# Nyström attention feeding a top-1 expert layer: attention's instruction order written out by hand, and the pseudo-inverse on 32x32 diagonal tiles

## Chip, cores, metric

One core of a Trainium2 chip runs the whole program in one launch. The metric is the device time in microseconds from launch to end; the median of several runs is compared. A profile of one execution shows what each engine did: TensorE (PE, with its weight loads apart as PEld), VectorE (DVE), ScalarE (ACT), GpSimd (POOL), SyncE (SP) and the DMA queues.

## What is computed

Attention for 8 batches, 8 heads, 576 tokens, head size 64, in f32, with 32 "landmarks" (means of 18 consecutive tokens), then a layer of 8 experts where each token goes to one.

```python
q_lm = q.reshape(B, H, 32, 18, D).mean(axis=3)      # k_lm likewise
A  = sm(q, k_lm); Bm = sm(q_lm, k_lm); C = sm(q_lm, k)   # softmax of scaled products
Z = Bm.T / (norm1(Bm) * norm_inf(Bm) + 1e-6)
for _ in range(6):
    Z = 2 * Z - Z @ Bm @ Z
x = A @ Z @ C @ v                                    # rows of 512: 8 heads x 64
logits = x @ w_gate;  e = argmax(logits)
out = softmax_prob(e) * sigmoid(x @ w_output_gate)[e] * (relu(x @ w1[e]) @ w2[e])
```

## The kernel before

**Units of work.** A batch is split into two halves of four heads (`hf`), so that 4 heads x 32 landmarks fill 128 partitions. There are 16 such half-batches, called units below. The program is written as a plain loop over batches and halves (L209, L213); the framework's scheduler decides in which order each engine gets the instructions, interleaving batches as buffers allow.

**Loads and turning (`turned`, L175 to L194).** q and k of a unit come by one DMA each on SP's queue (L178) into one of three buffers `nats` that borrow the space of the last expert's weights; v comes by three DMAs (L216). DVE turns the 32x32 blocks (L180). POOL sums 18 tokens to a landmark in five adds (L181 to L186) and spreads the landmarks with a mask into a block-diagonal matrix `bd` (L191), so that one 128x128 matmul serves four heads.

**Scores (`scores`, L196 to L207)**: four matmuls of 288 columns for C (L246) and for A (L268).

**Softmaxes.** C: maximum (L247), exponential on ACT (L250), transposes of the result (L257), copies (L258), times v (L262, 32-column tiles). A: DVE transpose out of PSUM (L270), maximum (L272), POOL subtracts (L276), ACT exponential (L277), DVE sum and reciprocal (L278, L279), POOL multiplies (L280), DVE transposes back into `AT` (L282). B: L225 to L243, with POOL writing it block-diagonal into `XW` (L235).

**Pseudo-inverse (L291 to L308).** Z is kept multiplied with C v: `XW` has, for each half, 128 columns of block-diagonal matrix and 64 of values, and seven steps each do one matmul of 192 columns per half (L295) and one DVE instruction (L299, L303, L306).

**Routing and output.** Z times the gate weights (L317 to L334), choice of expert (L336 to L350), ranks by counting (L353 to L368), a one-hot table `St` (L369), coefficients (L375 to L386). Token rows `x` come from ten matmuls of 256 columns per batch (L393), an ACT copy to bf16 (L396) and a store to DRAM (L397). Then positions are inverted into a list `gat_i` (L400 to L450).

**Expert weights** (`load_expert`, L75 to L82) are loaded by POOL's queue in f32 and cast to bf16 on the way, two DMAs an expert: expert b after batch b (b < 6), experts 6 and 7 after the last `AT`, because their space is borrowed till then.

**Experts (L452 to L522).** 43 tiles of 128 tokens: gather by an indirect DMA on POOL's queue (L464), transposes (L469), 8 matmuls (L483), ReLU (L487), transposes (L493), 8 matmuls (L502), scaling (L508), scatter (L509).

Of the kernel before, what the change touches and what calls it, by code (L numbers as in the profile page):

```python
# [22 lines left out]
F32 = mybir.dt.float32  # L23
BF16 = mybir.dt.bfloat16
EXP = mybir.ActivationFunctionType.Exp
SIG = mybir.ActivationFunctionType.Sigmoid
RELU = mybir.ActivationFunctionType.Relu
# [9 lines left out]
def kernel(  # L37
# [98 lines left out]
    s_bm = scale / (g * g)  # L136
    s_a = scale / g
    s_c = scale / g
    KC = g // 2
    NC = KC * m  # L140
    VJ = 6
    VA = g // VJ

    with tc.tile_pool(name="attn_c", bufs=1) as cp, \
# [17 lines left out]
        for G in Gs:  # L162
# [4 lines left out]
        nats = [wall[:, E - 1, i * 2 * GD:(i + 1) * 2 * GD].bitcast(F32).rearrange("p (k d) -> p k d", d=D)  # L167
                for i in range(3)]
        t9 = wall[:, E - 1, 6 * GD:7 * GD].bitcast(F32).rearrange("p (k d) -> p k d", d=D)
        VD = HH * VJ * D  # L170
        vSs = [wall[:VA * m, E - 2, i * 2 * VD:(i + 1) * 2 * VD].bitcast(F32).rearrange(
            "p (h j d) -> p h j d", h=HH, j=VJ) for i in range(2)]
        turns = iter(range(4 * B))

        def turned(src, b, hf):  # L175

            nat = nats[next(turns) % 3]
            nc.sync.dma_start(out=nat, in_=src[b, hf * HH:(hf + 1) * HH].rearrange("h (r k) d -> (h r) k d", k=g))  # L178
            tr = sb.tile([128, g, 2, m], F32, tag="tr", bufs=3)
            nc.vector.transpose(out=tr.rearrange("p k c r -> p (k c r)"), in_=nat.rearrange("p k d -> p (k d)"))  # L180
            nc.gpsimd.tensor_tensor(t9, nat[:, 0:9], nat[:, 9:18], op=ADD)  # L181
            nc.gpsimd.tensor_tensor(t9[:, 0:4], t9[:, 0:4], t9[:, 4:8], op=ADD)
            nc.gpsimd.tensor_tensor(t9[:, 0:2], t9[:, 0:2], t9[:, 2:4], op=ADD)
            nc.gpsimd.tensor_tensor(t9[:, 0], t9[:, 0], t9[:, 1], op=ADD)
            lm = sb.tile([128, D], F32, tag="lm")
            nc.gpsimd.tensor_tensor(lm, t9[:, 0], t9[:, 8], op=ADD)  # L186
            lmT = sb.tile([128, 2, m], F32, tag="lmT", bufs=4)
            nc.vector.transpose(out=lmT.rearrange("p c r -> p (c r)"), in_=lm)
            bd = sb.tile([128, 2, HH, m], F32, tag="bd", bufs=4)
            for c in range(2):  # L190
                nc.gpsimd.tensor_tensor(  # L191
                    bd[:, c], mask,
                    lmT[:, c, :].rearrange("p (h r) -> p h r", h=1).to_broadcast([128, HH, m]), op=MUL)
            return tr, lmT, bd  # L194

        def scores(bd, tr, tag, by_j=False):  # L196

            p = ps.tile([128, 2, 512], F32, tag=tag)
            for n in range(2):
                for c in range(2):  # L200
                    if by_j:
                        rhs = tr.rearrange("p (a j) c r -> p j a c r", j=VJ)[:, n * VJ // 2:(n + 1) * VJ // 2, :, c, :]
                    else:
                        rhs = tr[:, n * KC:(n + 1) * KC, c, :]
                    nc.tensor.matmul(p[:, n, :NC], lhsT=bd[:, c].rearrange("p h r -> p (h r)"),  # L205
                                     rhs=rhs, start=(c == 0), stop=(c == 1))
            return p[:, :, :NC]  # L207

        for b in range(B):  # L209
            XW = sb.tile([128, 2, 128 + D], F32, tag="X", bufs=3)  # L210
            cc = sb.tile([128, 2], F32, tag="cc")
            ATs = []
            for hf in range(2):  # L213
                vS = vSs[hf]
                for a in range(VA):
                    nc.sync.dma_start(  # L216
                        out=vS[a * m:(a + 1) * m],
                        in_=v[b, hf * HH:(hf + 1) * HH].rearrange("h (r k) d -> r h k d", k=g)[:, :, a * VJ:(a + 1) * VJ, :])
                qT, qlmT, qBD = turned(q, b, hf)
                kT, klmT, kBD = turned(k, b, hf)  # L220


                pB = ps.tile([128, 192], F32, tag="m", bufs=2)
                for c in range(2):
                    nc.tensor.matmul(pB[:, :m], lhsT=qBD[:, c].rearrange("p h r -> p (h r)"),  # L225
                                     rhs=klmT[:, c, :], start=(c == 0), stop=(c == 1))
                st = sb.tile([128, 8], F32, tag="st", bufs=4)
                nc.vector.tensor_reduce(st[:, 0:1], pB[:, :m], axis=X, op=MAX)
                nc.vector.tensor_scalar(out=st[:, 1:2], in0=st[:, 0:1], scalar1=-s_bm, scalar2=None, op0=MUL)
                Bm = sb.tile([128, m], F32, tag="Bm")  # L230
                nc.scalar.activation(out=Bm, in_=pB[:, :m], func=EXP, scale=s_bm, bias=st[:, 1:2],
                                     accum_out=st[:, 2:3])
                nc.vector.reciprocal(st[:, 3:4], st[:, 2:3])
                nc.vector.tensor_scalar(out=Bm, in0=Bm, scalar1=st[:, 3:4], scalar2=None, op0=MUL)
                nc.gpsimd.tensor_tensor(  # L235
                    XW[:, hf, :128].rearrange("p (h r) -> p h r", r=m), mask,
                    Bm.rearrange("p (h r) -> p h r", h=1).to_broadcast([128, HH, m]), op=MUL)
                pS = ps.tile([128, 192], F32, tag="m", bufs=2)
                nc.tensor.matmul(pS[:, :m], lhsT=bones, rhs=Bm)
                nc.vector.tensor_reduce(cc[:, hf:hf + 1], pS[:, :m], axis=X, op=MAX)  # L240
                nc.vector.tensor_scalar(out=cc[:, hf:hf + 1], in0=cc[:, hf:hf + 1], scalar1=1e-6,
                                        scalar2=None, op0=ADD)
                nc.vector.reciprocal(cc[:, hf:hf + 1], cc[:, hf:hf + 1])  # L243


                pC = scores(qBD, kT, "sc", by_j=True)  # L246
                nc.vector.tensor_reduce(st[:, 4:5], pC, axis=mybir.AxisListType.XY, op=MAX)  # L247
                nc.vector.tensor_scalar(out=st[:, 5:6], in0=st[:, 4:5], scalar1=-s_c, scalar2=None, op0=MUL)
                EC = sb.tile([128, VJ, VA * m], F32, tag="EC", bufs=1)
                nc.scalar.activation(out=EC.rearrange("p (n j) q -> p n (j q)", n=2), in_=pC, func=EXP,  # L250
                                     scale=s_c, bias=st[:, 5:6], accum_out=st[:, 6:7])
                nc.vector.reciprocal(st[:, 7:8], st[:, 6:7])
                ECT = sb.tile([VA * m, VJ, 128], F32, tag="ECT", bufs=1)
                for j3 in range(2):
                    pE = ps.tile([VA * m, VJ // 2, 128], F32, tag="et")
                    for j in range(VJ // 2):
                        nc.tensor.transpose(pE[:, j, :], in_=EC[:, j3 * (VJ // 2) + j, :], identity=I128)  # L257
                    nc.scalar.copy(ECT[:, j3 * (VJ // 2):(j3 + 1) * (VJ // 2), :], pE)  # L258
                pV = ps.tile([128, 192], F32, tag="m", bufs=2)
                for j in range(VJ):  # L260
                    for h in range(HH):
                        nc.tensor.matmul(pV[h * m:(h + 1) * m, :D], lhsT=ECT[:, j, h * m:(h + 1) * m],  # L262
                                         rhs=vS[:, h, j, :], start=(j == 0), stop=(j == VJ - 1))
                nc.vector.tensor_scalar(out=XW[:, hf, 128:], in0=pV[:, :D], scalar1=st[:, 7:8],
                                        scalar2=None, op0=MUL)


                pA = scores(kBD, qT, "sa")  # L268
                At = sb.tile([128, g, m], F32, tag="At")
                nc.vector.transpose(out=At.rearrange("p (n k) r -> p n (k r)", n=2), in_=pA)  # L270
                ax = sb.tile([128, 2, g], F32, tag="ax")
                nc.vector.tensor_reduce(ax[:, 0], At, axis=X, op=MAX)  # L272

                def b_l(ap):
                    return ap.rearrange("p (k r) -> p k r", r=1).to_broadcast([128, g, m])
                nc.gpsimd.tensor_tensor(At, At, b_l(ax[:, 0]), op=SUB)  # L276
                nc.scalar.activation(out=At, in_=At, func=EXP, scale=s_a)  # L277
                nc.vector.tensor_reduce(ax[:, 1], At, axis=X, op=ADD)  # L278
# [5 lines left out]
            if b < E - 2:  # L284
                load_expert(b, ATs[1])
            elif b == B - 1:
                load_expert(E - 2, ATs[1])
                load_expert(E - 1, ATs[1])
# [264 lines left out]
```

## Time and profile before

| | us |
|---|---|
| median of 3 runs (567.03 to 570.1) | 567.15 |
| the profiled execution: its time | 568.91 |
| its span, first to last instruction | 567.2 |
| PE / DVE / POOL / ACT busy in it | 438.5 / 285.8 / 305.1 / 122.0 |
| first expert transpose (L469) starts | 371.8 |

The profile has a line for each group of instructions: the source line, engine, operation, the tiles it writes and reads, the count, the busy time, the mean of one in ns, and the idle time of the engine before it with what ended that wait. A row of the timeline gives the start, the time from the first start to the last end, and the count. A row of stretches gives each engine's busy time between two moments. "PEclk" or clock is the granted share of TensorE's full clock.

### The profile page before, as it was taken

The numbers are of one execution on the slowest core, as the hardware profiler recorded it, in microseconds if no ns is written. First come the engines' busy times: TensorE is split into PE (matmuls) and PEld (weight loads), VectorE is DVE, ScalarE is ACT, GpSimd is POOL, SyncE is SP. The second block draws the span as 40 slices with busy tenths as digits, with TensorE's granted clock in tenths as the row PEclk, the third lists the DMA queues.
The fourth block names the chain that finished last, engine by engine and source line by source line (L and its number), as shares of the span: only waits on it lengthen the run. The fifth ranks groups of instructions, "written<-read, shape, count | busy, mean of one in ns | idle before, by whom it ended". The sixth has DMA issues, their size and how long they took to land. (4 is left out here: it accounts for less than half of the span.)

```text
span 567.2 us, 9257 instructions
## 1 busy us (share of the span) xinstructions
PE 438.5 (77%) x3127; PEld 277.0 (49%) x3127; DVE 285.8 (50%) x748; ACT 122.0 (22%) x279; POOL 305.1 (54%) x492
## 2 busy tenths in 40 slices
PE   0458758758776867779797878559999999999992
PEld 0235545536555545448474554325555555555551
DVE  1355557657666756736764322713444444353441
ACT  0012222123131222122231211112223222232220
POOL 2667895796687678585624111353444545454422
PEclk9978969969897958877897565769999999999998
DMA  6643946935989369388044754121232323223200
GB/s 163 168 125 84 210 119 180 213 107 118 254 195 206 100 167 218 103 156 184 9 111 68 126 92 72 33 75 57 75 112 85 107 81 104 86 92 94 85 29 0
DMA packets 41726, 66.13 MB, mean 117 GB/s; under 512 B 10353, under 2 KB 29810, under 8 KB 41682
## 3 DMA queue, kind: packets, MB, share of 16 engines
q0 software_dynamic: 18048, 31.90, 26.3%
q1 hardware_dynamic: 23634, 33.64, 21.5%
q8 instruction: 27, 0.44, 0.4%
q14 instruction: 17, 0.14, 0.1%
HBM read 67.58 MB, written 16.56 MB: 148 GB/s over the span
## 5 line engine op out<-in xcount | busy, mean ns | idle before, releaser
L205 PE MATMUL p<-tr,bd 128*128 128x288 f32 x256 | 88.6, 474 | 28.5 <-DVE tr L180 21.1
L509 POOL DMA_INDIRECT out_dram<-ysb x43 | 43.5, 1012 | 93.7 <-DVE ysb L508 90.0
L483 PE MATMUL ph<-wall,xT 128*128 x344 | 82.9, 385 | 3.0 <-DVE xT L471 2.9
L502 PE MATMUL py<-wall,hT 128*128 x344 | 81.1, 379 | 0.0
L393 PE MATMUL pX<-ZB,AT 128*128 128x256 f32 (+1 forms) x160 | 63.4, 520 | 19.8 <-ACT xo L396 15.2
L487 ACT ACTIVATE h<-ph 128x512 bf16<-128x512 f32 x86 | 46.7, 594 | 144.7 <-PE ph L483 141.6
L205 PEld LDWEIGHTS p<-tr,bd 128*128 128x128 f32 x256 | 52.9, 222 | 41.4 <-POOL bd L191 29.7
L295 PE MATMUL pN<-nxt 128*128 128x192 f32 x192 | 47.8, 375 | 19.9 <-DVE nxt L303 16.8
L483 PEld LDWEIGHTS <-xT 128*128 128x128 bf16 x344 | 33.9, 99 | 45.3 <-issue 5.7
L393 PEld LDWEIGHTS pX<-ZB,AT 128*128 128x128 f32 (+1 forms) x160 | 32.7, 233 | 44.1 <-ACT xo L396 23.1
L181 POOL TENSOR_TENSOR wall<-wall 128x576 f32<-128x576 f32 x32 | 44.9, 1402 | 13.7 <-DMA wall<-in_q_dram 11.3
L295 PEld LDWEIGHTS pN<-nxt 128*128 128x128 f32 x192 | 34.8, 209 | 33.7 <-DVE nxt L303 26.6
L464 POOL DMA_INDIRECT xs<-x_rows,gat_i x43 | 41.9, 974 | 15.9 <-issue 13.4
L180 DVE STREAM_TRANSPOSE tr<-wall 128x1152 f32<-128x1152 f32 x32 | 43.3, 1352 | 12.4 <-DMA wall<-in_q_dram 11.5
L502 PEld LDWEIGHTS <-hT 128*128 128x128 bf16 x344 | 31.9, 98 | 30.7
L495 DVE COPY hT<-pht 128x1024 bf16<-128x1024 bf16 x43 | 29.7, 690 | 29.4 <-PE pht L493 23.2
L507 DVE CAST ysb<-xs 128x1 int32<-128x1 f32 x43 | 6.6, 154 | 74.7 <-issue 64.6
L191 POOL TENSOR_TENSOR bd<-mask,lmT 128x128 f32<-128x128 f32 x64 | 28.0, 456 | 25.2 <-PE p L205 11.8
L508 DVE TENSOR_SCALAR ysb<-py,xs 128x512 f32<-128x512 f32 x43 | 31.9, 743 | 4.2 <-PE py L502 3.8
L396 ACT CAST xo<-pX 128x512 bf16<-128x512 f32 (+1 forms) x40 | 23.3, 581 | 49.9 <-PE pX L393 34.4
L303 DVE SCALAR_TENSOR_TENSOR nxt<-nxt,pN 128x384 f32<-128x384 f32 x40 | 21.5, 538 | 17.9 <-PE pN L295 17.7
L276 POOL TENSOR_TENSOR At<-At,ax 128x576 f32<-128x576 f32 x16 | 18.4, 1157 | 21.1 <-DVE ax L272 21.1
(136 smaller groups left out, 607.3 us busy)
## 6 DMA issues: line engine op xcount, KB each, us to landing
wall<-in_moe_w_dram POOLq DMA_DIRECT2D x16, 1024.0 KB
wall<-in_v_dram SPq DMA_DIRECT2D x48, 192.0 KB, 4.2
wall<-in_q_dram SPq DMA_DIRECT2D x16, 576.0 KB, 5.1
wall<-in_k_dram SPq DMA_DIRECT2D x16, 576.0 KB, 5.2
x_rows<-xo SPq DMA_DIRECT2D x32, 128.0 KB, 2.8
xs<-x_rows,gat_i POOLq DMA_INDIRECT x43
out_dram<-ysb POOLq DMA_INDIRECT x43
x_rows<-St SPq DMA_DIRECT2D x1, 516.0 KB, 4.6
```

Of the source, the lines that this page charges most:

```text
L180: nc.vector.transpose(out=tr.rearrange("p k c r -> p (k c r)"), in_=nat.rearrange("p k d -> p (k d)"))
L181: nc.gpsimd.tensor_tensor(t9, nat[:, 0:9], nat[:, 9:18], op=ADD)
L205: nc.tensor.matmul(p[:, n, :NC], lhsT=bd[:, c].rearrange("p h r -> p (h r)"), rhs=rhs, start=(c == 0), stop=(c == 1))
L295: nc.tensor.matmul(pN[:, hf, :], lhsT=cur[:, hf, :128], rhs=cur[:, hf, :])
L393: nc.tensor.matmul(pX[:tk, hf * HH * D:(hf + 1) * HH * D], lhsT=ATs[hf][:, j * 128:j * 128 + tk], rhs=ZB[:, hf].rearrange("p h d -> p (h d)"))
L464: nc.gpsimd.indirect_dma_start(out=xs, out_offset=None, in_=x_rows, in_offset=bass.IndirectOffsetOnAxis(ap=gat_i[:, j:j + 1], axis=0))
L483: nc.tensor.matmul(ph[hf], lhsT=xT[:, dc, :], rhs=wf[:, bass.ds(we[j] + (dc * F + hf * 512), 512)], start=(dc == 0), stop=(dc == DCH - 1))
L487: nc.scalar.activation(out=hs[j][:, hf * 512:(hf + 1) * 512], in_=ph[hf], func=RELU)
L495: nc.vector.tensor_copy(hTs[j], pht)
L502: nc.tensor.matmul(py, lhsT=hT[:, fc, :], rhs=wf[:, bass.ds(we[j] + (W1 + fc * HD), HD)], start=(fc == 0), stop=(fc == FCH - 1))
L508: nc.vector.tensor_scalar(out=ysb[:, :HD], in0=py, scalar1=xs[:, HD // 2:HD // 2 + 1], scalar2=None, op0=MUL)
L509: nc.gpsimd.indirect_dma_start(out=out, out_offset=bass.IndirectOffsetOnAxis(ap=token, axis=0), in_=ysb[:, :HD], in_offset=None, bounds_ch ...
```

## The change

1. Each step becomes a small function, and a list `plan` gives each call a place in time, in units of a period P = 12.0 a unit; the calls are sorted by place and issued under `manual_schedule`, so each engine's order is the program's. Loads of q and k are placed before those of v, for several units ahead, into six buffers (the space of experts 7 and 5); `AT` moves into seven slots of expert 4's space.
2. q and k are turned by TensorE (18 transposes a unit, `turn3`, copied by ACT, `keep3`) instead of DVE; landmarks too (`turn_lm`). The sums of q go to DVE, those of k stay on POOL. `bd` is gone.
3. Scores use 64x32 tiles: 8 matmuls of 288 columns, one per head and half of the contraction.
4. The pseudo-inverse has 96 columns a head and half (32 of matrix, 64 of values) in place of 192, with four 32x32 matmuls per half on the array's diagonal. B's softmax is done for both halves at once.
5. Experts 0 to 3 load after batches 0 to 3; experts 5, 6, 7 after the last `AT`; expert 4 last of all, after the last token rows.

The core of the diff:

```diff
+        nats = [home(E - 1 - i // 3 * 2, i % 3, GD).rearrange("p (k d) -> p k d", d=D) for i in range(6)]
+        def sums(u, i):
+            eng, t9, nat = (nc.gpsimd, nc.vector)[i], t9s[i], nats[(2 * u + i) % 6]
+            eng.tensor_tensor(t9, nat[:, 0:9], nat[:, 9:18], op=ADD)
+            eng.tensor_tensor(t9[:, 0:4], t9[:, 0:4], t9[:, 4:8], op=ADD)
+            eng.tensor_tensor(t9[:, 0:2], t9[:, 0:2], t9[:, 2:4], op=ADD)
+            eng.tensor_tensor(t9[:, 0], t9[:, 0], t9[:, 1], op=ADD)
+            lm[u, i] = sb.tile([128, 2, D], F32, tag=f"lm{i}", name="lm")
+            eng.tensor_tensor(lm[u, i], t9[:, 0:1].to_broadcast([128, 2, D]), t9[:, 8:9].to_broadcast([128, 2, D]), op=ADD)
+        def turn3(u, i, n):
...
+            tr[u, i, n] = pT = ps.tile([128, 3, 128], F32, tag="t", bufs=2, name="pT")
+            for k2 in range(3):
+                nc.tensor.transpose(pT[:, k2], identity=I128,
+                                    in_=nat[:, 6 * n + 2 * k2:6 * n + 2 * k2 + 2].rearrange("p k d -> p (k d)"))
+        def keep3(u, i, n):
+            nc.scalar.copy(tr[u, i][:, 3 * n:3 * n + 3], tr.pop((u, i, n)))
+        def scores(lms, tr, by_j=False):
+            p = ps.tile([128, 2, 512], F32, tag="s")
+            for h in range(HH):
+                for i in range(2):
+                    rhs = tr[i * D:(i + 1) * D, :, hm(h)]
...
+                    nc.tensor.matmul(p[hm(h), i, :NC], lhsT=lms[i * D:(i + 1) * D, hm(h)], rhs=rhs)
-                for hf in range(2):
-                    nc.tensor.matmul(pN[:, hf, :], lhsT=cur[:, hf, :128], rhs=cur[:, hf, :])
+        def p_mm(b, it):
+            pNs[b] = pN = ps.tile([128, 2, W + D], F32, tag="n", name="pN")
+            cur = XWs[b]
+            for hf in range(2):
+                for h in range(HH):
+                    nc.tensor.matmul(pN[hm(h), hf, :], lhsT=cur[hm(h), hf, :W], rhs=cur[hm(h), hf, :])
+        def a_back(u):
+            ATs[u] = home(E - 4, u % 7, S)
+            nc.vector.transpose(out=ATs[u], in_=Ats.pop(u).rearrange("p k r -> p (k r)"))
+        P = 12.0
+        for u in range(NU):
+            t = u * P
+            at(t - 4 * P + 11.9 if u > 2 else -30 + u, load_qk, u)
+            at(t - 2 * P + 11.9 if u > 1 else -30 + u + 0.5, load_v, u)
+            for n in range(3):
+                at(t - P + 1.5 + 0.4 * n, turn3, u, 0, n)
+                at(t - P + 2.6 + 0.5 * n, keep3, u, 0, n)
+                at(t - P + 4.9 + 0.4 * n, turn3, u, 1, n)
+                at(t - P + 5.5 + 0.5 * n, keep3, u, 1, n)
+            at(t - P + 0.1, sums, u, 0)
+            at(t - P + 1.9, sums, u, 1)
...
+            at(t + 0.0, c_scores, u)
+            at(t + 0.8, c_max, u)
+            at(t + 1.6, c_exp, u)
+            at(t + 3.5, a_scores, u)
...
+            at(t + P + 0.2, a_back, u)
...
+            for it, place in enumerate((0.7, 4.2, 7.8, 10.5, 12.7, 16.2, 19.8)):
+                at(t + place, p_mm, b, it)
+                at(t + place + 0.9, p_next, b, it)
...
+            for j, place in enumerate((6.9, 9.8, P + 2.8, P + 6.9, P + 9.7)):
+                at(t + place, x_mm, b, j)
+                at(t + place + 1.0, x_out, b, j)
+        for e in range(E):
+            u = 2 * e + 1 if e < E - 4 else NU - 1
+            at((NU + 4) * P if e == E - 4 else u * P + P + 3.3, lambda e=e, u=u: load_expert(e, ATs[u]))
+        with tc.manual_schedule():
+            for _, _, fn, args in sorted(plan, key=lambda p: p[:2]):
+                fn(*args)
```

## The prediction

> **What bounds the kernel now.** I read the page's head, then stretches of the span, then the chain's last part, then single lines.
>
> ```profile
> span 567.2 us, 9257 instructions
> 98.00:330.00 232.00, 174.31 (x1343) 123.69 (x1347) 140.85 (x391) 55.09 (x144) 145.48 (x265) 0.83 0.65 145
> 331.00:346.00 15.00, 11.19 (x43) 7.94 (x34) 3.80 (x8) 0.00 (x0) 1.70 (x2) 0.50 0.85 140
> 372.00:560.00 188.00, 181.13 (x1204) 96.68 (x1201) 78.87 (x171) 46.67 (x86) 82.09 (x84) 0.98 0.25 81
> ```
>
> The rows of stretches give from:to, length, then busy time of PE, weight loads, DVE, ACT, POOL, the granted clock, the DMA share and GB/s. From 372 us the experts run with PE busy 181 of 188 us at clock 0.98: that stage is PE-bound and the change leaves its code alone, so its 195.4 us (567.2 - 371.8, where 371.76 is its first transpose) stay. All before it is attention, and there no engine is full: in 98 to 330 PE has 75%, DVE 61%, POOL 63%, DMA 65%. The exponential of the C scores runs at 29.5 us for the first half-batch and at 321.7 for the sixteenth: 292.2 / 15 = 19.5 us of cadence, against a largest engine sum of 14.6 (0.75 x 19.5). So attention is bound by the order in which work reaches the engines, and the end by when the experts can begin.
>
> ```profile
> 165.78 0.88 PE L262 MATMUL pV<-wall,ECT 96*32 96x64 f32 x48
> 168.04 2.11 PE L205 MATMUL p<-tr,bd 128*128 128x288 f32 x8
> 342.70 1.65 PE L295 MATMUL pN<-nxt 128*128 128x192 f32 x4 [0.65 <-DVE nxt L303]
> 344.99 1.65 PE L295 MATMUL pN<-nxt 128*128 128x192 f32 x4 [0.65 <-DVE nxt L303]
> 347.02 0.47 PE L317 MATMUL pZ<-I,nxt 128*128 128x128 f32 x1 [0.38 <-DVE nxt L306]
> 371.76 0.58 PE L469 MATMUL pt<-Ib,xs 128*128 128x128 bf16 x4 [5.14 <-issue]
> ```
>
> Each f32 matmul is two instructions here. L205: 8 in 2.11 us, so 243 ns each from start to start once the last one's 0.41 us tail is taken off. L262: 48 instructions of 64 columns in 0.88 us, 14 ns each; alone, 64 of 288 columns would take 54. So four 32-column tiles run beside each other. The last three rows: an iteration of the last pseudo-inverse takes 2.29 us, and from its end to the experts lie 24.7 us.
>
> **Cadence after the change, engine by engine**, per half-batch ("unit"), each batch's work halved.
>
> *PE.* Gone: 16 score instructions (3.9 us), and half the columns of the pseudo-inverse. Added: 20 transposes of 128x128 (L257: 3 in 0.49 us, 109 ns each) = 2.2. Each of a unit's two score sets is now 16 instructions of 288 columns on 64x32 tiles: if all eight tiles run together 2 x 243 = 0.49 us, if only the four column groups do 0.97; twice a unit 1.0 to 1.9. Six transposes of EC 0.65, values 0.7. Per batch: seven iterations of 4 x 82 ns (half of L295's 163) = 2.3, token outputs 20 x 216 ns (L393) = 4.3, the small ones 1.0; half of 7.6 is 3.8. Sum 8.3 to 9.3. A change of tile shape costs: after a transpose the first L262 starts 202 ns later where the next transpose would start after 109, so 93 ns; some 22 changes a unit, 2.0 us. Total 10.3 to 11.3 at full clock, 12.4 to 13.6 at 0.83.
>
> *DVE.* The 1.35 us transposes (L180) go. Kept: L247 0.75, L270 0.77, L272 0.74, L278 0.75, reciprocals 0.4, L282 0.77 = 4.2. New: the sums of q come from POOL, five adds of 576, 256, 128, 64, 128 columns. Nearest rows with two SBUF inputs: L414 0.49 us for 320, L424 0.60 for 430; so 0.15 us + 1.05 ns a column, 1.95. Bounds: POOL's 3.4 for the same (L181 1.40 + 0.73 + 0.46 + 0.33 + 0.46), and 1.2 if the fixed part overlaps. Per batch: pseudo-inverse 2.3 (L303's 0.54 with half the columns is 0.34; six, and a last 0.28), routing lines L336 to L383 without waits 4.4, B softmax 1.5; half of 8.2 is 4.1. Sum 10.2.
>
> ```profile
> L345 DVE TENSOR_TENSOR w<-lg,sm x8: 199/439/1334, 70.0 to 352.4; 128x40 f32<-128x40 f32 x8
> L369 DVE TENSOR_TENSOR St<-row,psl x8: 806/930/1955, 84.7 to 356.8; 128x640 bf16<-128x640 f32 x8
> L181 POOL TENSOR_TENSOR wall<-wall 128x576 f32<-128x576 f32 x32 | 44.9, 1402 | 13.7 <-DMA wall<-in_q_dram 11.3 <-DMA wall<-in_k_dram 0.8
> ```
>
> Minimum/median/maximum: the same 40-column instruction takes 0.20 or 1.33 us, with POOL busy beside it, and L369 0.81 or 1.96. The longest excess, 1.15, is about one POOL instruction (L276 1.16, L181 1.40). Mean excess of L345, L349 and L369: 0.40, 0.33, 0.31, so 0.35 us per two-input instruction. The change has 8.5 of them a unit (five sums, seven per batch): 0 to 3.0 us, nearest the upper end, since sums of q and k now run side by side on the two engines. DVE: 10.2 to 13.2.
>
> The Trainium skill (SBUF — State Buffer, Who interferes with whom) says a DVE instruction with two SBUF inputs and a GpSimd instruction that reads SBUF exclude each other for their whole length. By it the 1.95 us and POOL's 3.4 us of sums add up rather than overlap, at most 1.95 us on either engine; the spread of L345 agrees. This speaks against moving a sum to DVE.
>
> *ACT* gets six copies of 384 columns (L258 0.47 each), 2.8; with L250 0.93, L277 0.68, two ECT copies 0.95, small 0.6 and half of 4.2 per batch: 8.1. *POOL* loses the bd products (4 x 0.46) and q's sums: 3.4 + 1.16 + 1.16 + half of 3.2, 7.3, and 1.0 more while experts load. *DMA* per unit: SP's queue took 21.5% of the span, 122 us, nearly all for attention: 7.6 for each of 16 units; one expert is 0.85 x 15 = 12.75 (second row above; the one expert loaded alone, 2.1 MB). Four experts in units 1 to 8: 7.6 + 6.4 = 14.0 there, 7.6 later; the loads are queued two units ahead, which covers it. SP's order changes too: token stores, for which SP now waits 133.7 us on ACT's copy, stand between loads that are wanted two units later, so a late store costs nothing up to that lead.
>
> The plan's places repeat every 12.0, but fix an order alone. So DVE about 12.5 to 13.2 and PE 11 to 13 stand level, both in fixed order: each finds its head instruction waiting at times (two PSUM tiles for all transposes: the third group of three waits for ACT's 0.47 us copy). I take 14.0 us, 94% for the fuller one; bounds 12.0 and 17.6 (13.2 at PE's present 75%).
>
> **Start, tail, sum.** First C exponential: k's load is now issued first, at 4.8 instead of 8.4; landing, sums 3.4, turning and scores give about 20 us (29.5 now). The sixteenth: 20 + 15 x 14 = 230 (321.7 now).
>
> After it, by rows, 9.6 us to the first iteration as now, seven iterations of 1.45 (2.29 less half of 4 x 0.32 at the half clock granted there, less 0.2 on DVE) = 10, then 24.7: experts at +44. But another wait is longer. The change lets experts 5, 6, 7 load only after the last AT (about +10: six DVE, POOL and ACT steps of 0.7 to 1.5), and expert 4 after the last token output. The first gather stands behind all four on POOL's DMA queue. That this queue goes in order is shown once: expert 7's two halves were issued at 331.9 and 332.7; packets of the first ran 333.4 to 339.4, of the second 339.1 to 345.0. So +10 + 1.5 + 4 x 12.75 + 3.1 (gather issue at 368.63 to L469) = +65.5. The cover which hid these loads, six of eight experts loaded during attention, is down to four.
>
> Experts begin at 20 + 15 x 14 + 65.5 = 295.5; end 295.5 + 195.4 = **491 us**. The profiled execution took 568.91 with a span of 567.2; the median of the runs is 567.15, equal to the span, so I compare spans with it.
>
> **Rivals.**
> - *The gathers do not wait for the weights* (other packets slip in, or loads run faster alone): +44 instead of +65.5, 469 us. For: DMA is only 14% busy in the tail. Against: the two halves above.
> - *Loose order*: the fuller engine reaches only 75% as now: 17.6 us, 281 + 264 = 545. For: every engine has strict order, so one late head holds all behind it.
> - *The tiles do not run side by side* (the change doesn't do what it says): 16 x 82 ns an iteration instead of 4 x 82, +0.98 us, 7 per batch, +3.4 per unit; PE 14.7, with waits 16.5: 528. For: no row shows four row groups together. Against: L262 for columns. The Trainium skill (TensorEngine Tiling (Array Packing), Restrictions and Gotchas) says different row tiles must not write one PSUM bank at a time, and pN is one bank: by it these would be taken in turn, 528, without it 491. No row before shows it.
> - *Slower: DVE blocked by POOL.* If each two-input instruction waits for a whole POOL one (1.2 us): 8.5 x 1.2 = 10.2, DVE 20.4, cadence 20.5: 588. It decides from 19.1 us ((567 - 281) / 15), that is 1.05 us per instruction. For: L345's maximum, and the sums now meet. Against: mean 0.35.
>
> **Chances.** Forecast 0.47 (12.5 to 15.5 us: 468 to 513); no wait 0.20; loose 0.13; tiles in turn 0.08; DVE blocked 0.12. A measurement can tell about 0.5% from no change. Slower: 0.10 of the last case; same 0.02 at the edge; faster 0.88. Range 450 to 548: below lies the no-wait case under 12.7 us (0.05), above half the loose case and the blocked one (0.17).
>
> **What would show it.** C exponentials 14 us apart; L345's successors with long maxima; sums on DVE near 2 to 3 us a unit; sixteen score instructions in 0.7 to 1.2 us; sixteen pN instructions in about 0.5; a DMA row near 0.85 with POOL's first gather landing only as the fourth expert ends; PE idle for some 20 us before L469's successor; then 195 us as before. Wrong if the cadence is above 16 or below 12, or if the first gather lands among weight packets.

## Result and profile after

The changed kernel takes **469.38 us** (median of 4 runs, 468.03 to 471.07) where the kernel before takes 568.62 (median of 4, 567.03 to 572.1): ratio 0.8249, 95% interval [0.8198, 0.8301]. The prediction said 491, in 450 to 548. The profiled execution took 468.03 with a span of 466.3, and the steps below are compared in spans.

The page of the changed kernel, its head and the slices of PE, the granted clock and DMA:

```profile
span 466.3 us, 11680 instructions
PE 378.6 (81%) x4401; PEld 223.2 (48%) x4423; DVE 259.6 (56%) x676; ACT 165.2 (35%) x383; POOL 227.2 (49%) x332
PE   0878877888788888887677349999999999999991
PEclk9887998999999999999775559999999999999997
DMA  6975999699797645221899950223223233323200
```

Each digit of a slice stands for 11.7 us. Read them from the left: nearly full clock through attention (the first 19 slices), then the tail, where DMA stands at 8 or 9 for four slices (20 to 23), the clock falls to 5 (22 to 24) and PE to 3 and 4 (23 and 24), then the experts as before. The stretches of the same kernel say it in microseconds (from:to, length, busy time of PE, weight loads, DVE, ACT, POOL, then clock, DMA share, GB/s; a share above 1 means that the times of the packets add up to more than the 16 engines' time):

```profile
133.00:200.00 67.00, 54.94 (x981) 35.69 (x982) 54.02 (x150) 37.63 (x98) 35.46 (x54) 1.00 0.59 155
212.00:265.00 53.00, 34.76 (x379) 21.03 (x378) 26.71 (x93) 11.44 (x30) 19.91 (x43) 0.72 0.94 167
265.00:272.00 7.00, 0.00 (x0) 0.00 (x0) 0.00 (x0) 0.00 (x0) 5.48 (x6) 0.50 1.19 242
272.00:466.00 194.00, 179.74 (x1182) 97.05 (x1204) 79.89 (x172) 46.67 (x86) 79.84 (x81) 0.97 0.24 76
```

In the steady part of attention PE and DVE now both stand at 81 to 82% and the clock at 1.00; before, 98 to 330 had 75%, 61% and 0.83. Then 53 us of tail with DMA at 0.94, and 7 us in which PE, DVE and ACT do nothing at all and POOL only issues gathers. The experts take 194 us as they did.

| step (spans, us) | before | predicted | after |
|---|---|---|---|
| first C exponential | 29.5 | 20 | 18.7 |
| 15 units of cadence | 19.5 each, 292.2 | 14.0 each, 210 | 12.87 each, 193.1 |
| sixteenth C exponential to experts | 50.1 | 65.5 | 60.4 |
| experts | 195.4 | 195.4 | 194.1 |
| sum | 567.2 | 491 | 466.3 |

Of the 100.9 us gained in span, cadence gave 99.1 and the start 10.8; the tail took 10.3 back, and the experts gave the last 1.3.

### The profile page after: what moved, and what is told of

It is laid out like the page before. It is cut to its first block, busy times and chain, and to the rows that moved or that the text cites. A ratio compares the mean times of both kernels' runs of the same rounds, so it can differ in the third digit from the quotient of the medians.

```text
span 466.3 us, 11680 instructions
## 1 busy us (share of the span) xinstructions
PE 378.6 (81%) x4401; PEld 223.2 (48%) x4423; DVE 259.6 (56%) x676; ACT 165.2 (35%) x383; POOL 227.2 (49%) x332
## 5 line engine op out<-in xcount | busy, mean ns | idle before, releaser
L210 PE MATMUL pT<-I,wall 128*128 128x128 f32 x288 | 49.7, 305 | 28.0 <-ACT tr L214 15.7
L214 ACT COPY tr<-pT 128x384 f32<-128x384 f32 x96 | 43.2, 479 | 39.7 <-PE pT L210 39.5
L210 PEld LDWEIGHTS pT<-I,wall 128*128 128x128 f32 x288 | 33.2, 151 | 41.9 <-ACT tr L214 25.5
L481 PE MATMUL pX<-ZB,wall 128*128 128x256 f32 (+1 forms) x160 | 49.8, 440 | 3.1 <-ACT xo L487 3.1
L290 POOL TENSOR_TENSOR At<-At,ax 128x576 f32<-128x576 f32 x16 | 18.5, 1158 | 53.4 <-DVE ax L287 53.4
L481 PEld LDWEIGHTS pX<-ZB,wall 128*128 128x128 f32 (+1 forms) x160 | 28.7, 201 | 14.2 <-issue 5.3
L661 PEld LDWEIGHTS <-h 128*128 128x128 bf16 x344 | 23.0, 98 | 11.0 <-issue 0.5
L300 POOL TENSOR_TENSOR At<-At,ax 128x576 f32<-128x576 f32 x16 | 18.5, 1156 | 19.4 <-DVE ZV L361 7.8
L349 PE MATMUL pN<-nxt 32*32 32x96 f32 x768 | 27.0, 258 | 0.5 <-DVE nxt L358 0.5
L197 POOL TENSOR_TENSOR wall<-wall 128x576 f32<-128x576 f32 x16 | 22.5, 1403 | 9.8 <-DMA wall<-in_k_dram 9.8
L661 PE MATMUL pht<-Ib,h 128*128 128x128 bf16 x344 | 26.7, 220 | 0.6 <-DVE hT L663 0.6
## 6 DMA issues: line engine op xcount, KB each, us to landing
wall<-in_moe_w_dram POOLq DMA_DIRECT2D x16, 1024.0 KB, 10.5
```

The lines of the kernel that those rows point to most:

```text
L210: nc.tensor.transpose(pT[:, k2], identity=I128, in_=nat[:, 6 * n + 2 * k2:6 * n + 2 * k2 + 2].rearrange("p k d -> p (k d)"))
L214: nc.scalar.copy(tr[u, i][:, 3 * n:3 * n + 3], tr.pop((u, i, n)))
L349: nc.tensor.matmul(pN[hm(h), hf, :], lhsT=cur[hm(h), hf, :W], rhs=cur[hm(h), hf, :])
L481: nc.tensor.matmul(pX[:tk(j), hf * HH * D:(hf + 1) * HH * D], lhsT=ATs[2 * b + hf][:, j * 128:j * 128 + tk(j)], rhs=ZBs[b][:, hf].rearrang ...
L661: nc.tensor.transpose(pht[:, fc, :], in_=h[:, fc * 128:(fc + 1) * 128], identity=Ib)
```

## Experiments

The kernel before was run again beside each set, and each ratio is to those runs. What is compared between experiments is the place in the span where the time changed.

### Does the fixed order make the gain?

```diff
-        with tc.manual_schedule():
-            for _, _, fn, args in sorted(plan, key=lambda p: p[:2]):
-                fn(*args)
+        for _, _, fn, args in sorted(plan, key=lambda p: p[:2]):
+            fn(*args)
```

> The changed kernel with the same small steps in the same program order, but the framework's scheduler, not the program, decides each engine's order. Theory 'order' (the fixed order is what closed the gaps): the cadence of the C exponentials goes back from 13.2 us to 16 or more, the experts begin 40 us later or more, 510 us or above. Rival 'work' (less and better spread work is what shortened it): 13 to 14.5 us, 465 to 490 us.

479.96 us, ratio 0.8436 [0.8376, 0.8496]. Cadence 13.26 in place of 12.87 (5.8 us over 15 units), experts at +65.4 in place of +60.4. That is the rival 'work': fixing the order is worth 10.6 us of the 99; the scheduler, given the same plan as program order, finds nearly the same.

### Are the diagonal tiles worth anything?

```diff
-    W = m
+    W = 128
...
-                for h in range(HH):
-                    nc.tensor.matmul(pN[hm(h), hf, :], lhsT=cur[hm(h), hf, :W], rhs=cur[hm(h), hf, :])
+                nc.tensor.matmul(pN[:, hf, :], lhsT=cur[:, hf, :W], rhs=cur[:, hf, :])
```

with B spread into blocks by POOL as in the kernel before.

> The changed kernel with the pseudo-inverse in the old form: block-diagonal 128x128, 192 columns a half, one full-array matmul per half. Per batch PE gets 7 x 0.32 = 2.3 us more, DVE 7 x 0.2 = 1.4, POOL two mask products, 1.06. If PE is what sets the steady cadence: +1.1 us a unit, 14.3 us, about +16 us, 485. If DVE: +0.7, +10 us, 479. If neither is full and the chains between engines set it: under +4 us, 473 or less.

470.59 us, ratio 0.8275 [0.822, 0.8329]: 1.2 us above the changed kernel, which these runs cannot tell from nothing. PE is busy 58.06 of 67 us between 133 and 200 instead of 54.94, some 0.6 us a unit; the cadence goes from 12.87 to 13.05.

### What do the late loads cost?

Three kernels change only when experts 4 to 7 are loaded. The first leaves these loads out (their tiles then use expert 3's weights, so that part of the output is not the reference's):

```diff
-        for e in range(E):
-            u = 2 * e + 1 if e < E - 4 else NU - 1
-            at((NU + 4) * P if e == E - 4 else u * P + P + 3.3, lambda e=e, u=u: load_expert(e, ATs[u]))
+        for e in range(E - 4):
+            u = 2 * e + 1
+            at(u * P + P + 3.3, lambda e=e, u=u: load_expert(e, ATs[u]))
...
-        nc.vector.tensor_scalar(out=tile_w[:, :J], in0=ej, scalar1=float(E - 1), scalar2=float(WE),
+        nc.vector.tensor_scalar(out=tile_w[:, :J], in0=ej, scalar1=float(E - 5), scalar2=float(WE),
```

> The changed kernel without the load of experts 4 to 7; tiles of those experts use expert 3's weights, so the matmul work is the same. Theory of the prediction (the first gather stands behind four experts on POOL's DMA queue, 21.5 us): the experts begin 15 to 21 us earlier, 449 to 455. By the trace of the changed kernel the gather is issued at 264.9 and its data are used at 272.2, 7.3 us against 3.1 before, so only 4.2 us of queue and up to 3 us of an interrupted POOL: 462. Rival 'the tail's own chain sets it, loads cost nothing': 467 to 470.

453.17 us, ratio 0.7951 [0.79, 0.8002]. Experts begin 45.8 us after the sixteenth C exponential (215.0), not 60.4: the loads cost **14.6 us** of tail. The timeline shows where. First POOL and PE of the changed kernel (start, time, engine, line, operation, in brackets the idle time before and what ended it):

```profile
226.51 0.75 POOL L80 DMA_DIRECT2D wall<-in_moe_w_dram  x1 [0.18 <-POOL wall L79]
227.25 0.89 POOL L82 DMA_DIRECT2D wall<-in_moe_w_dram  x1
228.15 1.32 POOL L418 TENSOR_TENSOR cum<-cum,oh 128x8 bf16<-128x8 bf16 x5
256.86 0.82 POOL L80 DMA_DIRECT2D wall<-in_moe_w_dram  x1 [1.49 <-issue]
258.59 1.77 POOL L596 TENSOR_TENSOR Va<-oj,row 128x430 bf16<-128x430 bf16 x2
264.92 1.06 POOL L632 DMA_INDIRECT xs<-x_rows,gat_i  x1 [3.10 <-issue]
```

```profile
229.25 0.19 PE L425 MATMUL prk<-cum,ones 128*128 128x40 bf16 x1 [3.40 <-POOL cum L418]
272.20 0.59 PE L637 MATMUL pt<-Ib,xs 128*128 128x128 bf16 x4 [9.29 <-DMA xs<-x_rows,gat_i]
```

and the same two engines without the loads:

```profile
257.68 1.07 POOL L632 DMA_INDIRECT xs<-x_rows,gat_i  x1 [3.11 <-issue]
```

```profile
231.33 0.18 PE L425 MATMUL prk<-cum,ones 128*128 128x40 bf16 x1 [0.87 <-POOL cum L418]
260.80 0.59 PE L637 MATMUL pt<-Ib,xs 128*128 128x128 bf16 x4 [5.14 <-issue]
```

From gather issue to first transpose it is 7.3 us (264.92 to 272.20) against 3.1, so 4.2 more. The other 10.4 us lie before the issue, which comes 53.1 us after the sixteenth C exponential instead of 42.7. The two are not separate prices: the packets of the four loads follow each other without a gap from 224.03 to 271.26, so by these figures a gather issued 10.4 us sooner would still have stood behind them. Two places of it show on POOL: six DMA issues of 0.75 to 0.90 us stand in front of the count (PE waits 3.40 us for it, not 0.87), and expert 4's two issues at 256.86 stand in front of the last routing steps. The clock is 0.72 between 212 and 265, against 0.90 without the loads (215 to 258). How the 10.4 divide among these, and the token stores that share the DMA engines with the weights, was not separated.

The next kernel issues expert 4's load in the round of the sixth expert tile instead of ahead of the first gather:

```diff
-            at((NU + 4) * P if e == E - 4 else u * P + P + 3.3, lambda e=e, u=u: load_expert(e, ATs[u]))
+            if e != E - 4:
+                at(u * P + P + 3.3, lambda e=e, u=u: load_expert(e, ATs[u]))
...
+            if j == 5:
+                load_expert(E - 4, tile_w[:, :1].bitcast(F32))
```

> The changed kernel, but expert 4's load is issued after the first gathers and a few scatters of the expert stage. Theory 'queue' (the first gather waits behind expert 4 on POOL's DMA queue, and POOL's last steps wait behind that load's issue): 4.2 us for the queue and about 3 for POOL's interrupted steps, the experts begin near 265 and the time is 462. Rival 'any load beside the token stores and the last batch costs, wherever it stands': no more than 2 us gained, 467 or above, since experts 5, 6 and 7 stay where they were.

479.18 us, ratio 0.8439 [0.8398, 0.848]. The experts do begin sooner, at +52.8, but take 210.5 us, 16.4 more. Waits of PE in the expert stage of this kernel (line, waited for, total, times, longest):

```profile
PE py L671 <- DMA wall<-in_moe_w_dram: 10.8, 1, 10.8
```

One wait of 10.8 us: the tiles at that place need other experts, but a matmul reads `wall` at an offset that is known only at run time, and the one that waits is the first that stands after the load in the program.

The third moves 5 and 7 to just before and just after the last C scores, 6 after the values, and leaves 4 in the expert stage:

```diff
+        at((NU - 1) * P - 1.0, lambda: load_expert(E - 3, ATs[NU - 3]))
+        at((NU - 1) * P + 1.0, lambda: load_expert(E - 1, ATs[NU - 3]))
+        at((NU - 1) * P + 11.0, lambda: load_expert(E - 2, ATs[NU - 2]))
...
+            if j == 5:
+                load_expert(E - 4, tile_w[:, :1].bitcast(F32))
```

> As the kernel before this one, and experts 7 and 5 are loaded when the last unit's q and k have been turned, some 20 us earlier, expert 6 after the last values. If the loads of the tail cost because POOL issues them (about 6 us) ahead of the count that the last batches wait for, and because their transfers stand beside the token stores, the experts begin within 4 us of the kernel without those loads (+46 to +50 us after the last C exponential, 453 to 458 us). If the loads only move their cost into the units before (DMA, POOL), the cadence of the last two units grows by what the tail gains: 461 or more.

477.97 us, ratio 0.8408 [0.8369, 0.8447]: experts at +50.2, and the same kind of wait, 10.5 us, for expert 4. The cadence of the last two units stays at 13.2. Over the four kernels the gather's issue moves with the loads that are left in the tail: +53.1 with four, +49.8 with three, +47.2 with two of these three issued 12 us sooner, +42.7 with none.

### Are the q sums rightly on DVE?

```diff
-            eng, t9, nat = (nc.gpsimd, nc.vector)[i], t9s[i], nats[(2 * u + i) % 6]
+            eng, t9, nat = (nc.gpsimd, nc.gpsimd)[i], t9s[i], nats[(2 * u + i) % 6]
```

> The changed kernel with the sums of q back on POOL: DVE loses 2.4 us a unit and meets POOL less, POOL goes from about 7.3 to 10.7 us of 13.2. If DVE and its waits for POOL set the cadence: 12 us or less, 450 to 455. If PE and its exchange with ACT set it: 13.0 to 13.4, 466 to 472. If POOL's longer chain (both sums before the landmarks can be turned) becomes the bound: above 13.6, 476 or more.

484.56 us, ratio 0.8496 [0.8439, 0.8553]: 15.2 us worse. The C exponentials come 12.1 to 12.2 and 15.4 to 17.7 us apart in turn. The stretch 98 to 200 of this kernel, and the largest row of DVE's waits in 133 to 200:

```profile
98.00:200.00 102.00, 83.60 (x1423) 53.68 (x1412) 59.27 (x166) 51.12 (x132) 80.10 (x133) 0.92 0.77 186
```

```profile
DVE At L284 <- PE p L234: 10.4, 5, 3.1
```

POOL goes to 80.10 us (58.66 in the same stretch of the changed kernel) and DVE falls from 80.77 to 59.27. DVE then waits for scores, which wait for landmarks from POOL. The clock drops to half for 3.4 to 6.8 us after every 23.9 us at full speed.

### Which engine sets the 13.2 us?

Dead work is added once per unit, to DVE (three reductions of a small constant, 1.2 us together) in one kernel, and to PE in another (each of k's nine transposes a second time, 0.98 us):

```diff
+        def extra():
+            for _ in range(3):
+                nc.vector.tensor_reduce(spare, mask64, axis=mybir.AxisListType.XY, op=MAX)
...
+            at(t + 4.5, extra)
```

> The changed kernel with three dead reductions of 256 columns on DVE in every unit, some 1.2 us. If DVE sets the cadence: 13.2 to 14.4 us, +17 us, 486. If DVE has slack there: under +0.3 us a unit, 469 to 474.

```diff
-            for k2 in range(3):
+            for k2 in (0, 1, 2) * (2 - i):
```

> The changed kernel with each transpose of k issued twice (the second writes the same data again): 9 x 0.109 = 0.98 us of PE a unit, nothing on the other engines. If PE sets the cadence: 14.2 us, +15 us, 484. If PE has slack (it waits for ACT's copies of the transposes anyway): under +0.4 us a unit, 469 to 475.

DVE: 472.49 us, ratio 0.831 [0.8264, 0.8356]; the units come 13.2 and 14.2 apart in turn. PE: 469.48 us, ratio 0.8257 [0.8213, 0.8301]; 13.2 and 13.6. So 1.2 us on DVE cost 1.0 in every second unit and nothing between, 0.98 us on PE at most 0.4 in every second. PE's waits in 133 to 200 show the slack, first of the changed kernel, then with the second transposes:

```profile
PE pT L210 <- ACT tr L214: 7.0, 11, 1.1
PE pM L219 <- ACT ECT L258: 2.5, 3, 0.8
PE pV L266 <- ACT ECT L258: 1.7, 2, 0.9
PE pE L253 <- ACT tr L214: 0.4, 2, 0.2
```

```profile
PE pT L210 <- ACT tr L214: 2.7, 10, 0.4
PE pV L266 <- ACT ECT L258: 1.7, 2, 0.9
PE pM L219 <- ACT ECT L258: 1.5, 3, 0.5
PE pE L253 <- ACT tr L214: 0.4, 2, 0.2
```

In the changed kernel PE is busy 54.94 us of 67 and waits 11.6 for ACT's copies: nothing else holds it. In the second, PE is busy 60.07 us, 5.1 more, and waits 6.3, 5.3 less: the added work filled the wait.

DVE is another case. In a unit of the sort that grew (in the changed kernel from the C exponential at 172.14 to that at 185.39) these waits form a ring:

```profile
179.00 1.31 POOL L418 TENSOR_TENSOR cum<-cum,oh 128x8 bf16<-128x8 bf16 x5 [0.83 <-DVE oh L412]
180.56 0.24 ACT L456 ACTIVATE wc<-wc 128x40 f32<-128x40 f32 x1 [0.66 <-POOL wc L452]
181.21 0.77 PE L266 MATMUL pV<-wall,ECT 96*32 96x64 f32 x40 [0.85 <-ACT ECT L258]
183.61 0.35 DVE L358 SCALAR_TENSOR_TENSOR nxt<-nxt,pN 128x192 f32<-128x192 f32 x1 [2.48 <-PE pN L349]
```

DVE, which has not stood idle since 171.3, chooses the experts (L412); on that wait POOL's count, then ACT, then PE, and at last DVE again. The dead reductions stand ahead of L412. They push it back by 1.23 us, L408 before it is 0.25 shorter (0.45 to 0.20, no longer beside POOL), and the 0.98 that remain come out whole: 14.23 for 13.25. In the other units POOL waits 6.2 us for the maximum of A (L287), and the reductions stand behind that. There they also move `St` (L443) out of the way of POOL's subtraction (L290, 165.35 to 166.51 in the changed kernel, where `St` runs from 165.45 to 167.19). With the reductions:

```profile
L443 DVE TENSOR_TENSOR St<-row,psl x8: 785/818/821, 86.2 to 248.1; 128x640 bf16<-128x640 f32 x8
```

0.82 us in place of 1.74, so DVE's way there grew by some 0.2 us, not 1.2, and slack on DVE in those units is not shown. Neither engine is full and neither sets the 13.2 alone. It is a chain through DVE, POOL, ACT and PE, on which DVE's steps lie: in the units that grew the 0.98 show it, in the others it is read from the waits alone.

### Is it the loads placed four units ahead?

```diff
-                nc.sync.dma_start(out=nats[(2 * u + i) % 6],
+                nc.sync.dma_start(out=nats[(2 * u + i) % 3],
...
-            at(t - 4 * P + 11.9 if u > 2 else -30 + u, load_qk, u)
+            at(t - 2 * P + 5.0 if u else -30, load_qk, u)
```

> The changed kernel with three buffers for q and k instead of six, each load issued some 7 us before its sums instead of 24. If the deep queue of loads carries the cadence (the DMA share is 0.96 while experts 0 and 1 load): the C exponentials of units 2 to 9 stand 3 to 6 us further apart, 490 to 515 us. If landing in 5 to 8 us is early enough: within 3 us of the changed kernel, 467 to 472.

470.21 us, ratio 0.828 [0.8203, 0.8358]; the same 13.2 to 13.6. Three buffers as before, loaded some 7 us ahead of their use, are enough.

### Does one part alone help the kernel before?

First the kernel before without `bd`, its score matmuls on 32x32 diagonal tiles of the landmarks themselves:

```diff
-            bd = sb.tile([128, 2, HH, m], F32, tag="bd", bufs=4)
-            for c in range(2):
-                nc.gpsimd.tensor_tensor(
...
-                    nc.tensor.matmul(p[:, n, :NC], lhsT=bd[:, c].rearrange("p h r -> p (h r)"),
-                                     rhs=rhs, start=(c == 0), stop=(c == 1))
+                    for h in range(HH):
+                        hs = slice(h * m, (h + 1) * m)
...
+                        nc.tensor.matmul(p[hs, n, :NC], lhsT=bd[hs, c, :], rhs=rhs, start=(c == 0), stop=(c == 1))
```

> The kernel before, with one part of the change in its own form: scores as 32x32 tiles on the diagonal straight from the turned landmarks, so that POOL's mask products (4 x 0.46 us a unit) go; DVE's turning, the sums on POOL and the scheduler's order stay. If those products stand on the chain that sets the old cadence of 19.5 us: 17.7 or less, 540 us or below. If they are hidden: 19 or more, 560 or above.

554.24 us, ratio 0.9784 [0.9704, 0.9865]; cadence 18.9, between the two cases. The second moves the sums of q to DVE as well:

```diff
+            eng, t9 = (nc.vector, t9b) if src is q else (nc.gpsimd, t9a)
```

> The kernel before this one, and the sums of q on DVE as in the change (POOL another 3.4 us less a unit, DVE 2.4 more). If POOL's part of the chain from load to scores sets the old cadence: 15 to 16.5 us, 500 to 520. If what is left (turning on DVE, three buffers for loads, the scheduler's order) sets it: 18 or more, 545 or above.

555.22 us, ratio 0.9804 [0.973, 0.9879]; cadence 19.3. Without `bd` the old structure gains some 12 us (2.2% of 567; by the interval 8 to 17). Moving the sums, worth 15 us in the new structure, gives nothing in the old.

### A version that beats both

All four late loads go earlier: 5 after the last sums, 7 after the last turns, 6 after the values, 4 after the token rows of the last batch but one; the last three `AT` get tiles of their own, so that expert 4's space is free in time.

```diff
-            ATs[u] = home(E - 4, u % 7, S)
+            ATs[u] = home(E - 4, u % 7, S) if u < NU - 3 else own[u % 3]
...
+        own = [cp.tile([128, S], F32, name=f"own{i}") for i in range(3)]
...
+        at((NU - 2) * P + 2.2, lambda: load_expert(E - 3, ATs[NU - 4]))
+        at((NU - 2) * P + 7.2, lambda: load_expert(E - 1, ATs[NU - 4]))
+        at((NU - 1) * P + 10.5, lambda: load_expert(E - 2, ATs[NU - 2]))
+        at((NU + 1) * P + 10.5, lambda: load_expert(E - 4, ATs[NU - 1]))
```

> The changed kernel with all late loads issued earlier and apart: expert 5 after the last sums, 7 after the last transposes of q and k, 6 after the last values, 4 after batch 6's token rows (the last three AT get tiles of their own, so its space is free). By the kernel without those loads (experts at +45.8 us after the sixteenth C exponential instead of +60.4) and by the one with expert 4's load inside the expert stage (PE stood 10.8 us for it): if the loads end before the first gather and POOL issues them where nothing waits, the experts begin at +46 to +50, 453 to 459 us. If loads beside the last units cost there what they save later: 463 or above.

**459.01 us**, ratio 0.8088 [0.8037, 0.8139], 10.4 below the changed kernel. Experts begin at +44.9; the tail of this kernel:

```profile
217.00:259.00 42.00, 27.10 (x381) 17.03 (x379) 26.83 (x94) 11.52 (x30) 16.87 (x35) 0.94 1.10 194
```

The DMA engines carry at least as much as in the changed kernel's tail (1.10 against 0.94), and the clock is 0.94: the loads end at 255.5, before the gathers, and two of the four are issued ahead of the sixteenth C exponential. The first gather is issued at +41.4, so full DMA engines alone are not what delayed it to +53.1. The last unit pays for it, 16.1 us long instead of 13.2.

## Why the prediction was right, and where its sizes were off

**Bound before, start, experts.** Attention was held by more than its fullest engine, as read: 4.9 of the 19.5 us a unit lay above the largest engine sum (14.6); now 2.4 of 13.2 lie above it (10.8). So the sums gave 3.8 of the gain and fewer waits 2.5. Part of the 3.8 is the granted clock, 0.83 under the 14.6 and 1.00 under the 10.8; the two were not separated. The start came at 18.7 (20 predicted). The experts took 194.1 (195.4).

**Cadence: the term that was mis-sized**, 15 x 1.13 = 16.9 of the 24.7 us. The engine sums per unit, from the stretch 133 to 200 times 13.2 / 67: PE 10.8 (10.3 to 11.3 predicted at full clock), ACT 7.4 (8.1), POOL 7.0 (7.3), DVE 10.6 (10.2 to 13.2). The miss is DVE's, where the upper end was taken for what POOL's neighbourhood costs, 3.0 us a unit. Lines of the changed kernel show what it cost (minimum/median/maximum in ns):

```profile
L408 DVE TENSOR_TENSOR w<-lg,sm x8: 200/451/964, 69.6 to 242.7; 128x40 f32<-128x40 f32 x8
L443 DVE TENSOR_TENSOR St<-row,psl x8: 783/1740/1741, 85.5 to 248.1; 128x640 bf16<-128x640 f32 x8
L198 DVE TENSOR_TENSOR wall<-wall x16: 424/560/836, 14.4 to 199.5; 128x256 f32<-128x256 f32 x16
```

The sums on DVE take 2.46 us a unit (2 to 3 predicted), against 1.98 if each of the five ran at its fastest; L443 is over its fastest by 0.72 on average and L408 by 0.33, 0.36 and 0.17 a unit, as each comes once a batch. Together 1.0, not 3.0. Beside that, the fuller engine was to be busy 94% of the time; PE and DVE are at 82 and 81%. That error goes the other way: 10.8 / 0.82 = 13.2 stands against 13.2 / 0.94 = 14.0. So it is in part luck that the cadence was missed by no more than 1.1 us. And the step itself, a fixed share of the fuller engine, is not how the 13.2 come about: as far as the runs show, the chain above sets them, and 0.98 us more on PE hardly moved it. The mean is lower still, 12.87, because the first units come about 11.2 us apart.

The Trainium skill (SBUF — State Buffer, Who interferes with whom) spoke against moving the sums, since DVE and POOL would exclude each other. The spread of L443 and L198 agrees that they meet, and `St` fell from 1.74 to 0.82 us where the dead reductions kept it from POOL's subtraction. But the whole toll is 1.0 us a unit, and undoing the move costs 15.2 us in all.

**Tiles side by side.** Sixteen pN instructions and sixteen score instructions of the changed kernel:

```profile
156.57 0.53 PE L349 MATMUL pN<-nxt 32*32 32x96 f32 x16
157.04 0.72 PE L234 MATMUL p<-tr,lmT 64*32 64x288 f32 x16
```

0.53 and 0.72 us, as foreseen (about 0.5, 0.7 to 1.2). Eight score instructions start within 46 ns and their second passes 266 ns later; the four row groups of pN start 7 ns apart. The Trainium skill (TensorEngine Tiling (Array Packing), Restrictions and Gotchas) forbids different row tiles to write one PSUM bank at a time. For tiles on the diagonal, each in its own 32 partitions, no turn-taking shows here, and the rival built on it is refuted. That the tiles run side by side does not mean that they gain: the block-diagonal form, with twice the columns, is as fast within 1.2 us.

**The tail.** Right in its mechanism, 5.1 us too long (its terms add up to 65.6, not 65.5): last `AT` at +8.7 (10), the four loads in 47.2 us (224.03 to 271.26), not 51, since each one's first packets start before the one before has ended. That the gather stands last behind them holds: its first packet is at 270.06, the matmul at 272.20. Without the loads +45.8 was measured, where the rival had +44. What the prediction did not see is that the same loads also delay the gather's issue by 10.4 us, so that mending the queue's order alone would win only 4.2; an earlier issue alone would, by the packets, win nothing.

**The other rivals.** Loose order (17.6): false, 12.87 with the fixed order and 13.26 without. DVE blocked by POOL (20.4): false.

**What stays open.** Undone one at a time, the parts give 10.6 us (fixed order), 15.2 (sums), 1.2 (diagonal tiles), 0.8 (early loads): 28 of 99. What remains is turning on PE instead of DVE, the 64x32 scores without `bd` (some 12 us in the old structure), and the plan's program order, which lays each unit's front part over the back part of those before it, where the kernel before goes batch by batch. PE's waits of before in 98 to 330 fit the last:

```profile
PE pX L393 <- ACT xo L396: 13.5, 10, 4.3
PE pN L295 <- DVE nxt L303: 11.3, 15, 1.8
PE prk L356 <- DVE oh L350: 6.7, 2, 6.4
PE pS L239 <- DVE Bm L234: 6.5, 5, 4.0
```

They are waits on whole-batch steps (token rows, pseudo-inverse, routing, the softmax of B), single ones up to 6.4 us, and none of them is left among those of the changed kernel above. How the rest divides among the three was not tried. So it is not shown that the program order is the largest part.

## What to carry to other kernels

When no engine is full, look at what each waits for: here the waits on whole-batch results went, only short waits on copies were left, and 9% more PE work then cost almost nothing. Dead work on an engine tests the place where it stands: ahead of a hand-over that others wait for it came out whole, behind it not, and it can shorten a neighbour by moving it. Price a moved load at the place where it lands, with its issues, which stand in front of the engine's own work, and with the queue behind it. A load that is read at a run-time offset must be issued where no reader follows soon: one such load held the expert stage for 10.8 us.

## What the runs showed of the hardware

- DVE's two-input instructions lose less beside a busy POOL than their longest cases suggest: L408's maximum is 0.964 us for an instruction that takes 0.200 at its fastest, yet the whole toll is 1.0 us a unit. `St` (L443) takes 1.74 us where POOL's L290 (1.16) runs over its start, and 0.82 once 1.2 us of other DVE work stands between them.
- With PE busy 82% and its waits at most 1.1 us, the granted clock was 1.00 through 133 to 200. With sums back on POOL, PE is as busy (83.60 of 102 us, 83.80 in the changed kernel), but the clock was half for 3.4 to 6.8 us after every 23.9 (0.92 in the stretch). That the length of the waits decides was not tested.
- Consecutive 2.1 MB loads on POOL's queue overlapped at their ends: four in 47.2 us, where one takes 12.2 to 13.3 from its first packet to its last.
